# The order of batch 1's transpositions, of the w_out loads and of GpSimd's first sums in a fused attention and MoE kernel

## The chip, the cores and the metric

The kernel runs on one NeuronCore of a Trainium2 chip. The metric is the device time of one execution in microseconds (us); the figure compared is the median of several executions. Engines are named as in the profile: PE (TensorE), PEld (its weight loads), DVE (VectorE), ACT (ScalarE), POOL (GpSimd) and SP (SyncE, which here only issues DMAs).

## The reference

For each of 8 batches and 8 heads, `x` (512 x 64) and `state` (32 x 64) attend to each other. With `scale = 1/sqrt(64)`:

```
a      = softmax(scale * x @ state.T)    # 512 x 32
xread  = a @ state
a2     = softmax(scale * state @ x.T)    # 32 x 512
sread  = a2 @ x
rows   = concat([xread, sread])          # 544 rows a batch, heads side by side: 512 wide
out    = leaky_relu(rows @ w_in, 0.01) @ w_out     # w_in 512 x 2048, w_out 2048 x 512
```

The output has 8 * 544 = 4352 rows of 512 values in fp32.

## The kernel before, in words

**Tiling.** All products run on bf16 operands with fp32 sums. A batch is transposed so that the features lie on the partitions: the tile `xT`. Its scores `sc` (`a_scores`, line 252) are 8 small matmuls on parts of the array. The matrix `M` is `state @ w_in` for one batch, so that the first MoE layer is `M` against the first probabilities `aT`. `M` is made in four column blocks (`a_m`, line 409, and `m_evict`, line 429). The first layer is `ff1` (line 439): two matmuls for each of the 16 row blocks `s`, into a PSUM bank `ph`, and a leaky ReLU on ACT that writes a block of `hT`. The second layer is `piece(b, hT, i, jq, js)` (line 541): for row tile `i`, matmuls over the blocks `4*jq + js` of `hT` and `w_out`, one for each block, into a bank `py` or `pyw`. Line 1005 names `half`, the two halves (0, 1) and (2, 3) of such a quarter.

**Softmax of one batch.** For the first probabilities DVE runs `a_shift` (the maxima `mrow`, line 266; their spread `sh`, line 274; the difference, line 280), ACT runs the exponential (`a_exp`, line 284), DVE runs `a_recip` (lines 289 to 298) and `a_probs` (line 302), which writes `aT`. For the second probabilities DVE runs `a_max2` (line 341), ACT `a_exp2` (line 347, with the row sums) and DVE `a_probs2` (lines 355 to 365), which writes `a2`.

**Order.** There is no scheduler: each engine runs its instructions in the order in which the code issues them, and waits on semaphores. Nothing on an engine passes a waiting instruction, but weight loads may be issued ahead of the matmuls that they belong to.

**Stages around the change.** Batch 0 has its own path (lines 871 to 992). While its `hT` (`h0`) is multiplied by `w_out` in `piece`s, batch 1 (`a1`) is prepared: its `x`, loaded in two halves `x1[0]` and `x1[1]` (line 876), is cast to bf16 on DVE (line 995), transposed on PE by 8 small matmuls for each half into a PSUM tile `pxt2` (line 1015) and copied to `xT` on DVE (line 1018). Then come `a_scores(a1)`, the softmax of batch 1, and from line 1066 on the loop of `ff1(a1, h1, s)`, which needs `aT` of batch 1 and carries the rest of batch 0's `piece`s between its steps.

Batch 2's `x` comes in two halves `xl` and is cast on ACT (line 126, called at line 1041); each half is then transposed by a DMA that SP issues (`a_xt_half`, line 239). The states of batches 2 and 3 are loaded by 8 DMAs of SP (`load_state(0)`, line 199, which follow a memset of two columns, line 999), cast on POOL (`state_cast(0)`, line 208) and transposed by a third DMA of SP (`state_t(0)`, line 213). `a_scores(a2)` at line 1077, step 4 of the loop, needs all three of these.

**Queues.** `w_in`, `w_out` (with a cast from fp32 to bf16), `x1` and `xl` are loaded by DMAs that POOL issues (lines 144 to 156 and 871 to 885), and they land in the order of their issue. Later loads, transposing DMAs and the output are issued by SP. POOL also forms differences of blocks of `w_out` (`tw_sum`, line 577), of which `tw_sum(1, ...)` at line 1029 needs `w_out` tiles 0 to 7.

Of the kernel before, what the change touches and what calls it, by code (L numbers as in the profile page):

```python
# [9 lines left out]
P = 128  # L10
B, H, S, D = 8, 8, 512, 64
# [4 lines left out]
NT = S // P  # L16
NK = H // 2
SCALE = 1.0 / (D ** 0.5)

BF16 = mybir.dt.bfloat16  # L20
# [7 lines left out]
def kernel(  # L28
# [9 lines left out]
    nc = tc.nc  # L38

    consts = ctx.enter_context(tc.tile_pool(name="consts", bufs=1))  # L40
# [6 lines left out]
    psum = ctx.enter_context(tc.tile_pool(name="psum", bufs=2, space=bass.MemoryType.PSUM))  # L47
# [5 lines left out]
    VEC, SCA, POO = nc.vector.tensor_copy, nc.scalar.copy, nc.gpsimd.tensor_copy  # L53
# [18 lines left out]
    ident = consts.tile([P, P], BF16, name="ident")  # L72
# [47 lines left out]
    def pair_of(a, t, k):  # L120
        h = 2 * (k % 2)
        return a.xb[k // 2][:, t, h:h + 2, :].rearrange("p h d -> p (h d)")
# [27 lines left out]
    def load_w_out_rows(j0, j1):  # L150
        nc.gpsimd.dma_start(
            w_out_bf[:, j0:j1, :], moe_w_out[P * j0:P * j1, :].rearrange("(j p) f -> p j f", p=P)
        )

    def load_w_out(c):
        load_w_out_rows(4 * c, 4 * (c + 1))
# [39 lines left out]
    stf = [consts.tile([P, hi - lo, P], FP32, name=f"stf{lo}") for lo, hi in groups]  # L196
    stb = [consts.tile([P, hi - lo, P], BF16, name=f"stb{lo}") for lo, hi in groups]

    def load_state(i):
        lo, hi = groups[i]  # L200
        for k in range(NK):
            for g in range(2):
                nc.sync.dma_start(
                    stf[i][NS * k:NS * (k + 1), :, D * g:D * (g + 1)],
                    state[lo:hi, 2 * k + g].rearrange("b n d -> n b d"),
                )
# [38 lines left out]
    def st_of(a, g, k):  # L245
        rows = slice(D * g, D * (g + 1))
        if a.b == 0:
            return stbd[rows, k, g ^ (k // 2), :]
        t = st1 if a.b == 1 else st_t[0][:, a.b - 2] if a.b < 4 else st_t[1][:, a.b - 4]
        return t[rows, NS * k:NS * (k + 1)]  # L250

    def a_scores(a):
        sc = psum.tile([P, 2, S], FP32, name="sc", tag="sc", bufs=1)
        for k in range(NK):
            for g in range(2):
                nc.tensor.matmul(  # L256
                    sc[NS * k:NS * (k + 1), g, :],
                    lhsT=st_of(a, g, k),
                    rhs=a.xTh[k // 2][D * g:D * (g + 1), :, k % 2, :],
                    start=True, stop=True,  # L260
                )
        a.sc = sc
# [52 lines left out]
    def a_shift(a):  # L315
        a_max(a)
        a_diff(a)
# [36 lines left out]
    def a_probs2(a):  # L354
        nc.vector.tensor_scalar(out=a.r2[:], in0=a.r2[:], scalar1=1e-9, scalar2=None, op0=ALU.add)
        q2 = att.tile([P, 2], FP32, name="qc", tag="qc")
        nc.vector.reciprocal(q2[:], a.r2[:])
        if a.b in (0, 6):
            pairs[a.b] = att.tile([P, 2, 2, S], BF16, name="a2p", tag="a2p", bufs=1)
        if a.b in (0, 1, 6, 7):  # L360
            a.a2 = pairs[a.b - a.b % 2][:, a.b % 2]
        else:
            a.a2 = att.tile([P, 2, S], BF16, name="a2", tag="a2", bufs=1)[:]
        for g in range(2):
            nc.vector.tensor_scalar(
                out=a.a2[:, g, :], in0=a.e2[:, g, :],
                scalar1=q2[:, g:g + 1], scalar2=None, op0=ALU.mult,
            )
# [172 lines left out]
    def piece(b, hT, i, jq, bank=None, copy=SCA, js=range(4)):  # L541
        if jq == 0 and js[0] == 0:
            y = ys[b, i] = Y()
            y.py = psum.tile([P, DM], FP32, name="py", tag="py")[:] if bank is None else bank
        y = ys[b, i]
        for j in [4 * jq + v for v in js]:
            nc.tensor.matmul(  # L547
                y.py, lhsT=hT[:, j, P * i:P * (i + 1)], rhs=w_out_bf[:, j, :],
                start=(j == 0), stop=(j == 15),
            )  # L550
        if jq == 3 and copy is not None:
            y_store(b, i, copy)

    def y_store(b, i, copy):
        tag = ("ysb", "s1", "ysb", "s6")[i]
        ysb = ypool.tile([P, DM], FP32, name="ysb", tag=tag, bufs=3 if tag == "ysb" else 1)
        copy(ysb[:], ys[b, i].py)
        nc.sync.dma_start(rows_of(b)[i], ysb[:])
# [5 lines left out]
    def tw_open():  # L564
        for n in (1, 2):
            t = consts.tile([P, HJ, HN], BF16, name=f"tw{n}", tag=f"x1{n - 1}")
            tw[n] = [t[:, 4 * u:4 * (u + 1)] for u in range(2)]
        for n in (3, 4):
            tw[n] = []
            for u in range(2):  # L570
                t = consts.tile([P, 4, HN], BF16, name=f"tw{n}", tag=f"xf{2 * (n - 3) + u}")
                tw[n].append(t[:])
# [199 lines left out]
    a0, a1, a2 = att_of[:3]  # L772
# [102 lines left out]
    for u in range(2):  # L875
        nc.gpsimd.dma_start(
            x1[u][:], x[1, NK * u:NK * (u + 1)].rearrange("h (p t) d -> p h (t d)", t=NT)
        )
    load_w_out_rows(2, 4)
    load_w_out(1)  # L880
    load_w_out(2)
    load_x_half(2, 0)
    load_w_out_rows(12, 14)
# [52 lines left out]
    h0 = hpool.tile([P, 16, S], BF16, name="hT", tag="hT")  # L936

    def open_ff1_0(tag):
        if tag in ("sc", "big"):
            pr = psum.tile([P, 2, S], FP32, name="php", tag=tag, bufs=1)  # L940
            return pr, [pr[:, 0], pr[:, 1]]
        ph = [psum.tile([P, S], FP32, name="ph", tag=tag) for _ in range(2)]
        return ph, [p[:] for p in ph]
# [39 lines left out]
    for j, tag in ((4, "ph"), (6, "big"), (8, "py"), (10, "big"), (12, "py"), (14, "ph")):  # L983
        t, bk = open_ff1_0(tag)
# [5 lines left out]
        elif j == 8:  # L990
            a_scores(a0)
            m_halves(a0, 3, "ph")
            a_max2(a0)
    for u in range(2):
        VEC(
            a1.xb[u].rearrange("p t h d -> p h t d"),
            x1[u][:].rearrange("p h (t d) -> p h t d", t=NT),
        )
    nc.vector.memset(stf[0][:, 0, D - 1:D + 1], 0.0)
    load_state(0)  # L1000

    for g in range(2):
        a_exp2(a0, g)
    wide = psum.tile([P, 2, DM], FP32, name="pyw", tag="big", bufs=1)
    half = (range(0, 2), range(2, 4))
    for u in range(2):
        piece(0, h0, 2 + u, 0, bank=wide[:, u], js=half[0])
    for i in (0, 1):
        piece(0, h0, i, 0, js=half[0])
    for u in range(2):  # L1010
        ps = psum.tile([P, NT, 2, P], BF16, name="pxt2", tag="ph")
        for t in range(NT):
            for v in range(2):
                h = NK * u + 2 * v
                nc.tensor.transpose(
                    ps[:, t, v, :], pair_of(a1, t, h // 2), ident[:]
                )
        VEC(a1.xT[:, :, 2 * u:2 * u + 2, :], ps[:])
    for i in (2, 3):
        piece(0, h0, i, 0, js=half[1])  # L1020
    a_scores(a1)
    m_evict(a1, 1, a_m(a1, 1, "ph"), SCA)
    for i in (0, 1):
        piece(0, h0, i, 0, js=half[1])
    a_probs2(a0)
    a_shift(a1)
    a_max2(a1)
    tw_open()
    for j in (4, 6, 0, 2):
        tw_sum(1, j, j + 2, nc.gpsimd)  # L1030
    for i in (0, 1):
        piece(0, h0, i, 1)
    pm = a_m(a1, 2, "ph")
    a_exp(a1)
    m_evict(a1, 2, pm, SCA)
# [93 lines left out]
    for b in range(2, B):  # L1129
# [22 lines left out]
        for s in range(16):  # L1152
# [75 lines left out]
            if b == 7 and s in FA_AT:  # L1228
                i = FA_AT.index(s)
# [49 lines left out]
    for n in (1, 2, 6, 5, 7, 3, 4):  # L1279
        two_product(q, n)  # L1280
        if n in (3, 4):
            u = n - 3
# [43 lines left out]
```

## Time and profile before

| what | us |
|---|---|
| median of 3 executions | 202.36 (202.03 to 202.39) |
| the profiled execution | 202.76 |
| its span, from the first to the last instruction | 201.0 |
| PE busy in the span | 195.4 (97%) |
| DVE busy | 158.7 (79%) |
| ACT busy | 141.9 (71%) |
| POOL busy | 72.6 (36%) |

All times in traces count from the first instruction of the program. In the timeline, a row is a run of like instructions on one engine: start, length from the first start to the last end, engine, line, operation, output and input, number, and in brackets the idle time before it with what ended it. The length that a matmul shows includes its way through the array, so that neighbouring matmuls overlap in the rows; their distance is that of their starts. The chain of waits leads from the last instruction back through whatever released each step; there each row holds the time that counts towards the end. The DMA view gives for each issue the size and the time from issue to landing.

### The profile page before, as it was taken

What the parts mean: (1) busy time and instruction counts of PE and PEld (TensorE: products, weight loads), DVE (VectorE), ACT (ScalarE), POOL (GpSimd) and SP (SyncE); (2) the same over time, 40 slices, a digit from 0 to 9 for tenths busy, and PEclk for the clock granted to TensorE, in tenths of its full rate; (3) what the DMA queues carried; (4) which work ended last, traced back from release to release, by engine and by line L of the source; (5) the groups of instructions that cost most, each with busy time, mean ns of one, the idle gap of its engine ahead of it and who ended that gap; (6) DMA issues with size and microseconds to landing.
All of it is one profiled execution on the core that took longest, in us unless ns stands there. A gap on an engine that the chain in (4) does not pass through costs nothing.

```text
span 201.0 us, 4628 instructions
## 1 busy us (share of the span) xinstructions
PE 195.4 (97%) x1880; PEld 130.1 (65%) x1880; DVE 158.7 (79%) x241; ACT 141.9 (71%) x274; POOL 72.6 (36%) x76
## 2 busy tenths in 40 slices
PE   7998999999999999999999999999999999999993
PEld 3643534443476767776776677676767777799982
DVE  3665799399999989985999889898999945984712
ACT  3678738899889868766887779777868555757420
POOL 8823272992091373037300760054004600540000
PEclk9999999999999999999999999999999999999999
DMA  6999998697999944852473404220025302210115
GB/s 198 207 207 297 212 290 147 119 346 170 196 219 228 308 49 72 237 216 55 88 225 139 128 16 92 104 109 0 0 104 157 58 0 104 108 49 8 52 38 170
DMA packets 38773, 27.75 MB, mean 138 GB/s; under 512 B 24416, under 2 KB 35808, under 8 KB 38752
## 3 DMA queue, kind: packets, MB, share of 16 engines
q1 hardware_dynamic: 33584, 20.78, 39.3%
q0 software_dynamic: 4832, 6.29, 15.4%
q10 hardware_dynamic: 336, 0.39, 0.8%
q8 instruction: 14, 0.23, 0.5%
q14 instruction: 7, 0.06, 0.1%
HBM read 17.30 MB, written 8.91 MB: 130 GB/s over the span
## 4 chain that ended last, share of the span: by engine, by line
PE 91%; DMA 3%; DVE 2%; ACT 1%; ACTq 1%; SPq 0%; issue 0%
PE ph L442 24%; PE ppx L642 18%; PE ppb L642 15%; PE py L547 7%; PE ppr L699 6%; PE pm L421 4%; PE pyw L547 3%; PE pf L520 3%; PE ppw L642 3%; DMA xf<-in_x_dram 2%; PE psr L394 2%; PE php L947 1%; PE ph L947 1%; PE sc L256 1%; DMA out_dram<-ysb 1%; DVE m L830 1%
## 5 line engine op out<-in xcount | busy, mean ns | idle before, releaser
L447 ACT ACTIVATE hT<-ph 128x512 bf16<-128x512 f32 x112 | 66.7, 605 | 25.2 <-PE ph L442 24.5
L442 PE MATMUL ph<-aT,M 128*128 128x512 bf16 x224 | 65.5, 380 | 0.0
L607 POOL TENSOR_TENSOR S<-hT,S 128x512 bf16<-128x512 bf16 x24 | 32.1, 1357 | 82.2 <-DVE S L607 55.5
L642 PEld LDWEIGHTS <-S 128*128 128x128 bf16 x384 | 37.0, 98 | 12.7 <-issue 0.9
L642 PEld LDWEIGHTS <-hT 128*128 128x128 bf16 x288 | 28.0, 98 | 11.1
L607 DVE TENSOR_TENSOR S<-hT 128x1024 bf16<-128x1024 bf16 x24 | 25.0, 1069 | 3.3 <-ACT hT L447 3.3
L442 PEld LDWEIGHTS <-M 128*128 128x128 bf16 x224 | 20.9, 98 | 8.8 <-issue 2.9
L642 PE MATMUL ppx<-tw,S 128*128 128x256 bf16 x160 | 20.8, 273 | 0.0
L547 PEld LDWEIGHTS <-hT 128*128 128x128 bf16 x96 | 9.1, 98 | 11.4 <-issue 1.0
L547 PE MATMUL py<-w_out_bf,hT 128*128 128x512 bf16 x64 | 16.0, 380 | 0.0
L739 DVE TENSOR_TENSOR ysb<-ppb,s 128x512 f32<-128x512 f32 x12 | 8.3, 692 | 6.2 <-PE ppb L642 6.1
L642 PE MATMUL ppb<-tw,S 128*128 128x256 bf16 x96 | 12.4, 273 | 0.0
L642 PE MATMUL ppb<-w_out_bf,hT 128*128 128x256 bf16 x96 | 12.4, 273 | 0.0
L642 PE MATMUL ppb<-w_out_bf,S 128*128 128x256 bf16 x96 | 12.3, 273 | 0.0
L435 ACT CAST M<-pm 128x1024 bf16<-128x1024 f32 x11 | 11.2, 1018 | 0.3 <-PE pm L421 0.3
L642 PE MATMUL ppx<-w_out_bf,hT 128*128 128x256 bf16 x80 | 11.2, 273 | 0.0
L347 ACT ACTIVATE e<-sc,mcol 128x512 bf16<-128x512 f32 x16 | 11.1, 700 | 0.0
L586 POOL TENSOR_TENSOR tw<-w_out_bf 128x512 bf16<-128x512 bf16 x8 | 9.0, 1153 | 4.2 <-DMA w_out_bf<-in_moe_w_out_dram 4.2
L642 PE MATMUL ppx<-tw,hT 128*128 128x256 bf16 x80 | 10.4, 273 | 0.0
L341 DVE TENSOR_REDUCE mcol<-sc 128x2 f32<-128x1024 f32 x8 | 9.7, 1214 | 0.0
L266 DVE TRANSPOSE_TENSOR_REDUCE mrow<-sc 128x32 f32<-128x1024 f32 x7 | 8.7, 1242 | 1.2 <-PE sc L256 1.2
L132 POOL CAST xb<-xl 128x2048 bf16<-128x2048 f32 x5 | 9.5, 1892 | 0.0
(148 smaller groups left out, 322.5 us busy)
## 6 DMA issues: line engine op xcount, KB each, us to landing
out_dram<-ysb SPq DMA_DIRECT2D x11, 512.0 KB, 2.6
xl<-in_x_dram SPq DMA_DIRECT2D x5, 1024.0 KB, 6.4
out_dram<-ysb SPq DMA_DIRECT2D x9, 256.0 KB, 4.7
w_in_bf<-in_moe_w_in_dram POOLq DMA_DIRECT2D x4, 512.0 KB, 9.8
xf<-in_x_dram SPq DMA_DIRECT2D x4, 256.0 KB, 3.7
w_out_bf<-in_moe_w_out_dram POOLq DMA_DIRECT2D x4, 256.0 KB, 13.6
x<-in_x_dram POOLq DMA_DIRECT2D x2, 512.0 KB, 14.6
w_out_bf<-in_moe_w_out_dram POOLq DMA_DIRECT2D x2, 512.0 KB, 16.5
```

Source lines behind the costliest of these rows:

```text
L132: nc.gpsimd.tensor_copy(xt[b][:].rearrange("p t h d -> p h t d"), xl[b][:].rearrange("p h (t d) -> p h t d", t=NT),)
L266: nc.vector.tensor_reduce(out=m1[:], in_=flat.rearrange("p (c j) -> p c j", j=NS), axis=AX.X, op=ALU.max, apply_transpose=True,)
L341: nc.vector.tensor_reduce(out=a.m2[:], in_=a.sc[:], axis=AX.X, op=ALU.max, negate=True)
L347: nc.scalar.activation(out=a.e2[:, g], in_=a.sc[:, g, :], func=AF.Exp, bias=a.m2[:, g:g + 1], accum_out=a.r2[:, g:g + 1],)
L435: copy(a.M[:, :, cols], pm[:])
L442: nc.tensor.matmul(ph[:], lhsT=a.M[:, g, P * j:P * (j + 1)], rhs=a.aT[:, g, :], start=(g == 0), stop=(g == 1),)
L447: nc.scalar.activation(out=hT[:, j, :], in_=ph[:], func=AF.Prelu, scale=1 / SCALE, alpha=0.01)
L547: nc.tensor.matmul(y.py, lhsT=hT[:, j, P * i:P * (i + 1)], rhs=w_out_bf[:, j, :], start=(j == 0), stop=(j == 15),)
L586: eng.tensor_tensor(out=tw[n][u][:, at], in0=in0, in1=in1, op=ALU.subtract)
L607: eng.tensor_tensor(out=part(n), in0=in0, in1=in1, op=op)
L642: nc.tensor.matmul(q[bank][v], lhsT=lhsT, rhs=w_of(n, j), start=q["open", bank] and j == 0, stop=j == 7, skip_group_check=True,)
L699: nc.tensor.matmul(q.bank[w], lhsT=lhsT, rhs=w_of(n, j), start=n in (1, 2, 5) and j == 0, stop=j == HJ - 1, skip_group_check=True,)
```

## The change

Four things move; no arithmetic changes.

1. The loads of `w_out` on POOL's queue. Before, tiles 2 and 3 followed both halves of batch 1's `x`, and tiles 4 to 7 came as one DMA. Now tiles 2 and 3 lie between the two halves of `x`, tiles 4 and 5 follow the second half, and tiles 6 and 7 are a DMA of their own.
2. The cast, the 8 transposing matmuls and the copy of each half of batch 1's `x` are three functions, and the two halves are no longer issued together: the first half's transpositions follow the first eight `piece` matmuls; then come all eight of `half[1]` of the first quarter, the second half's transpositions, four matmuls of the second quarter, and only then `a_scores(a1)`.
3. On DVE, the memset of `stf[0]` (which SP's eight loads of `load_state(0)` wait for) follows the first copy, the second half's cast follows that, and `a_probs2(a0)` lies between the second half's cast and its copy.
4. POOL copies one element of batch 0's second probabilities into a new tile `behind` before its first `tw_sum`, so that these sums wait until `a_probs2(a0)` is done.

The counts of matmuls, of DVE and of ACT instructions stay the same. POOL has one DMA issue and one copy more.

```diff
@@ -876,8 +876,8 @@
             x1[u][:], x[1, NK * u:NK * (u + 1)].rearrange("h (p t) d -> p h (t d)", t=NT)
         )
-    load_w_out_rows(2, 4)
-    load_w_out(1)
+        load_w_out_rows(2 + 2 * u, 4 + 2 * u)
+    load_w_out_rows(6, 8)
     load_w_out(2)
@@ -991,14 +991,26 @@
-    for u in range(2):
+    def x1_cast(u):
         VEC(
             a1.xb[u].rearrange("p t h d -> p h t d"),
             x1[u][:].rearrange("p h (t d) -> p h t d", t=NT),
         )
-    nc.vector.memset(stf[0][:, 0, D - 1:D + 1], 0.0)
-    load_state(0)
-
+
+    def x1_t(u):
+        ps = psum.tile([P, NT, 2, P], BF16, name="pxt2", tag="ph")
+        for t in range(NT):
+            for v in range(2):
+                h = NK * u + 2 * v
+                nc.tensor.transpose(
+                    ps[:, t, v, :], pair_of(a1, t, h // 2), ident[:]
+                )
+        return ps
+
+    def x1_copy(u, ps):
+        VEC(a1.xT[:, :, 2 * u:2 * u + 2, :], ps[:])
+
+    x1_cast(0)
     for g in range(2):
         a_exp2(a0, g)
@@ -1007,29 +1019,27 @@
     for i in (0, 1):
         piece(0, h0, i, 0, js=half[0])
-    for u in range(2):
-        ps = psum.tile([P, NT, 2, P], BF16, name="pxt2", tag="ph")
-        for t in range(NT):
-            for v in range(2):
-                h = NK * u + 2 * v
-                nc.tensor.transpose(
-                    ps[:, t, v, :], pair_of(a1, t, h // 2), ident[:]
-                )
-        VEC(a1.xT[:, :, 2 * u:2 * u + 2, :], ps[:])
-    for i in (2, 3):
+    x1_copy(0, x1_t(0))
+    nc.vector.memset(stf[0][:, 0, D - 1:D + 1], 0.0)
+    load_state(0)
+    x1_cast(1)
+    a_probs2(a0)
+    for i in (2, 3, 0, 1):
         piece(0, h0, i, 0, js=half[1])
+    x1_copy(1, x1_t(1))
+    for i in (0, 1):
+        piece(0, h0, i, 1, js=half[0])
     a_scores(a1)
     m_evict(a1, 1, a_m(a1, 1, "ph"), SCA)
-    for i in (0, 1):
-        piece(0, h0, i, 0, js=half[1])
-    a_probs2(a0)
     a_shift(a1)
     a_max2(a1)
     tw_open()
+    behind = consts.tile([1, 1], BF16, name="behind")
+    nc.gpsimd.tensor_copy(behind[:], a0.a2[:1, 1, S - 1:])
     for j in (4, 6, 0, 2):
         tw_sum(1, j, j + 2, nc.gpsimd)
     for i in (0, 1):
-        piece(0, h0, i, 1)
+        piece(0, h0, i, 1, js=half[1])
     pm = a_m(a1, 2, "ph")
     a_exp(a1)
```

## The prediction

> **What bounds the kernel now.** I read the page first: PE is the engine that carries the span.
>
> ```profile
> PE 195.4 (97%) x1880; PEld 130.1 (65%) x1880; DVE 158.7 (79%) x241; ACT 141.9 (71%) x274; POOL 72.6 (36%) x76
> ```
>
> So the change can gain only where PE waits, and it loses wherever it makes PE wait. Next the chain of waits around the changed lines (start, us that count towards the end):
>
> ```profile
> 21.47 0.86 PE pyw L547 x4
> 22.33 0.86 PE py L547 x4
> 23.19 0.89 PE pxt L1015 x16
> 24.09 0.86 PE pyw L547 x4
> 24.95 0.47 PE sc L256 x8
> 25.41 0.22 PE pm L421 x8
> 25.63 2.69 PE py L547 x12
> ...
> 35.68 0.86 PE ph L442 x4
> ```
>
> From 21.47 to 35.68 it never leaves PE. A `piece` matmul counts 0.86/4 = 0.216 us, a transposition 0.89/16 = 0.056. So I look for steps that are longer than their like. The timeline of PE (starts) has one, batch 1's scores against batch 2's:
>
> ```profile
> 23.92 1.03 PE L547 MATMUL pyw<-w_out_bf,hT 128*128 128x512 bf16 x4
> 24.88 0.54 PE L256 MATMUL sc<-xT,st 64*32 64x512 bf16 x8
> 25.56 0.39 PE L547 MATMUL py<-w_out_bf,hT 128*128 128x512 bf16 x1
> ```
> ```profile
> 39.50 0.41 PE L256 MATMUL sc<-xT,st_t 64*32 64x512 bf16 x8
> 40.05 0.39 PE L442 MATMUL ph<-aT,M 128*128 128x512 bf16 x1
> ```
> ```profile
> 35.52 0.38 PE L442 MATMUL ph<-aT,M 128*128 128x512 bf16 x1
> ```
>
> Scores and the block of M behind them take 25.56 - 24.88 = 0.68 for batch 1 and 40.05 - 39.50 = 0.55 for batch 2: 0.13 is lost. DVE tells why:
>
> ```profile
> 22.52 0.69 DVE L995 CAST xb<-x 128x1024 bf16<-128x1024 f32 x1 [0.56 <-DMA x<-in_x_dram]
> 23.68 1.29 DVE L1018 COPY xT<-pxt 128x1024 bf16<-128x1024 bf16 x2 [0.45 <-PE pxt L1015]
> 24.88 0.16 DVE L355 TENSOR_SCALAR r<-r 128x2 f32<-128x2 f32 x1
> 25.81 1.24 DVE L266 TRANSPOSE_TENSOR_REDUCE mrow<-sc 128x32 f32<-128x1024 f32 x1
> 33.87 0.69 DVE L302 TENSOR_TENSOR aT<-e,qb 128x1024 bf16<-128x1024 bf16 x1
> ```
>
> The second copy to `xT` ends at 23.68 + 1.29 = 24.97, just behind the scores' start at 24.88. **That 0.13 is all there is to gain here.** The reader should also note the last two rows: batch 1's softmax starts on DVE at 25.81 and `aT` is there at 33.87 + 0.69 = 34.56, while `ff1(a1)` starts on PE at 35.52. Less a semaphore of some 0.05 (the copy's end at 24.97 to the scores' second half), the slack is 0.91.
>
> **Part 1, the loads.** Issues on POOL's queue and their times to landing (rows in pairs):
>
> ```profile
> 7.56 0.79 POOL L876 DMA_DIRECT2D x<-in_x_dram  x1
> x<-in_x_dram POOLq DMA_DIRECT2D x1, 512.0 KB, 14.9
> 8.31 0.75 POOL L151 DMA_DIRECT2D w_out_bf<-in_moe_w_out_dram  x1
> w_out_bf<-in_moe_w_out_dram POOLq DMA_DIRECT2D x1, 256.0 KB, 15.3
> 9.85 0.78 POOL L151 DMA_DIRECT2D w_out_bf<-in_moe_w_out_dram  x1 [0.79 <-DMA w_in_bf<-in_moe_w_in_dram]
> w_out_bf<-in_moe_w_out_dram POOLq DMA_DIRECT2D x1, 512.0 KB, 16.3
> ```
>
> The second half of x lands at 22.5, tiles 2-3 at 23.6, tiles 4-7 at 26.15: 1.1 to 1.25 us for two tiles. With the same bytes in another order, tiles 2-3 land near 22.2, the second half of x at 23.6, tiles 4-5 at 24.85, tiles 6-7 at 26.15. POOL's extra issue costs it 0.75 at a time when it waits for older transfers anyway (idle 0.79 in the row above).
>
> [...]
>
> **Part 2, PE's order.** I lay the instructions out anew with the starts of before. The eight first `piece` matmuls end their slots at 23.03 as before (the 16 transpositions, 0.89, follow them and end where `pyw` starts, at 23.92). Then: 8 transpositions to 23.48, 8 matmuls (1.73) to 25.21, 8 transpositions to 25.65, 4 matmuls (0.86) to 26.52, the change to small tiles (24.88 less 23.92 + 4 x 0.216 = 0.09), **scores at 26.61**, 1.73 later than now. What each step needs is there: tiles 2-3 (22.2 against 23.48), tiles 4-5 (24.85 against 25.65), tiles 6-7 (26.15 against about 27.6).
>
> **Part 3, DVE's order.** The first copy starts at 23.68 as now and a copy holds DVE for about 0.61 (the two 1.29, less an overlap of 0.08); memset; the second cast at 24.34, with x since 23.6; it ends at 25.03, 0.15 ahead of its transpositions. `a_probs2(a0)` then holds DVE from 24.95 for 25.81 - 24.88 = 0.93, to 25.88. The second group of transpositions ends at about 25.85, so the copy runs from 25.88 to 26.57. The scores at 26.61 need not wait: the 0.13 goes. But the maxima follow the scores: batch 2 has its maxima here:
>
> ```profile
> 39.98 1.25 DVE L266 TRANSPOSE_TENSOR_REDUCE mrow<-sc 128x32 f32<-128x1024 f32 x1 [1.22 <-PE sc L256]
> ```
>
> That is 39.98 - 39.50 = 0.48 behind the scores' start, so for batch 1 they come at 26.61 + 0.48 = 27.09, **1.28 later than 25.81**: before, DVE was behind on the probabilities and hid part of PE's order; now PE is late. From there the chain is serial (maxima, spread, difference, exponential, sums, reciprocal, spread, product) and nothing in it was waiting for anything else, so `aT` moves from 34.56 to 35.84. PE, 0.13 early, would want `ff1(a1)` at 35.39 and gets it at 35.84 + 0.05 = 35.89 to 35.91: a wait of 0.52, and **+0.39 against before**. This wait holds the loop's first matmul, and on PE's in-order queue all of `ff1`, batch 0's last pieces and batch 2's scores behind it.
>
> **Behind it: ACT and SP.** ACT runs the exponential, then M, then the casts of batch 2's x:
>
> ```profile
> 29.62 1.06 ACT L284 ACTIVATE e<-sh 128x1024 bf16<-128x1024 f32 x1 [2.88 <-DVE sh L280]
> 31.52 1.06 ACT L126 CAST xb<-xl 128x1024 bf16<-128x1024 f32 x1
> 33.41 1.04 ACT L126 CAST xb<-xl 128x1024 bf16<-128x1024 f32 x1 [0.83 <-DMA xl<-in_x_dram]
> 36.15 1.09 ACT L447 ACTIVATE hT<-ph 128x512 bf16<-128x512 f32 x2 [0.34 <-PE ph L442]
> ```
>
> The exponential moves by 1.28 and the first cast with it, to end at 33.86; the second only to 33.77-34.81, since it used to wait 0.83 for its transfer. Before, ACT was done with what lies between that cast and the first ReLU at 36.15 - 0.34 = 35.81; now, 0.36 later, at 36.17, and the ReLU comes at 36.15 + 0.39 = 36.54: hidden. SP's three transposing DMAs follow:
>
> ```profile
> 32.60 2.05 SPq L240 DMA_TRANSPOSE xT<-xb  x1
> 34.76 1.24 SPq L240 DMA_TRANSPOSE xT<-xb  x1
> 36.10 1.19 SPq L214 DMA_TRANSPOSE st_t<-stb  x1
> st_t<-stb SPq DMA_TRANSPOSE x1, 2.9
> q0 software_dynamic: 30, 0.03, 10.2%
> 89.45 1.23 SPq L372 DMA_TRANSPOSE a2T<-a  x1
> 39.49 0.11 PEld L256 LDWEIGHTS <-st_t 64*32 64x32 bf16 x8 [0.42 <-DMA st_t<-stb]
> ```
>
> The states land at 36.10 + 2.9 = 39.0, and PE wants them at 39.49 (its 0.42 idle is the usual change of tiles, not a wait): slack 0.49. In the changed kernel PE wants them at 39.88. Their issue stands third in SP's queue: 33.88, plus the first issue, plus 1.24, plus 0.21 of semaphores (34.76 - 34.65 and 36.10 - 36.00). The first took 2.05 where an equal one with a quiet queue took 1.23 (row of 89.45): two ends for a cost that I cannot settle. With 1.23 the states land at 33.88 + 1.23 + 1.24 + 0.21 + 2.9 = 39.46, in time; with 2.05 at 40.28, and PE waits 40.33 - 39.88 = 0.45 more. From 33.0 to 34.7 the DMA view still shows the last 30 packets of POOL's queue (q0) beside it; 1.28 later they are gone, so I take 1.23.
>
> **Part 4, POOL.** `behind` waits for the probabilities, done near 25.96, when tiles 4-5 are there and 6-7 about to be: the sums start near where tiles 4-7 let them start before, and their reader on DVE stands behind the product for `aT`: nothing. The memset comes 1.2 later (24.3 for 23.2), and SP's state loads with it; POOL casts what they bring:
>
> ```profile
> 32.85 0.86 POOL L209 TENSOR_SCALAR stb<-stf 128x256 bf16<-128x256 f32 x1 [2.06 <-DVE qh L296]
> ```
>
> It ended at 33.71, ends at 34.9 if all of the 1.2 comes through, and is wanted by the third issue at 33.88 + 1.23 + 1.24 + 0.21 = 36.56: hidden.
>
> **Sum.** -0.13 (scores) + 0.52 (`aT`) = +0.39 on PE from 35.5 on. After that PE is dense and the order is unchanged, so the shift reaches the end. The profiled execution would go from 202.76 to 203.15. The median of the runs is 0.40 lower than that execution: 202.36 + 0.39 = **202.75**.
>
> **Rivals.**
>
> *The states are late too.* The first transposing issue keeps its 2.05. Total +0.39 + 0.45 = +0.84: 203.2. For: the row does not say what held that issue, and 30 packets are few. Against: the quiet 1.23.
>
> *Faster.* If `w_out` comes more slowly in ordinary executions than in the profiled one, the kernel before waits for tiles 4-7, which PE wants at about 26.44 and which land at 26.15, while the changed one wants tiles 4-5 only (0.8 of slack) and 6-7 at 27.6. With these 1.2 later, before loses 0.9 and the changed kernel still 0.39: 202.36 - 0.5 = 201.9 in relative terms. It decides from a landing later than 26.15 + 0.29 + 0.39 = 26.8. Against: no PE wait for `w_out` in the trace, and three runs within 0.36.
>
> *The change does not do what it says.* `aT` is later by less, or the slack of 0.91 is larger by jitter of either, and PE only sheds its 0.13: 202.2 to 202.5.
>
> *The split costs a landing.* If the extra DMA delayed all behind it by a step of its own, 1.1 to 2.5 us as between the landings above, batch 2's second half would land at 34.5 to 35.9 and its cast end 1.05 later, at 35.55 to 36.95, where the second transposing issue would go at 35.22. The states then land 0.33 to 1.73 later, at 39.8 to 41.2, and PE waits up to 1.35 for them: 202.75 to 204.1. The landings speak against it. [...]
>
> **Chances.** Forecast 0.53 (own range 202.55 to 203.0); states late 0.24; faster 0.08; no effect 0.13; the split's landing 0.02. A measurement can tell about 0.2%, 0.4 us, from no change. The forecast lies at that edge: half of it counts as slower, half as within. Slower: 0.27 + 0.24 + 0.02 = 0.53; within: 0.26 + 0.13 = 0.39; faster 0.08. The range takes in the forecast, the states' delay and most of "no effect": 202.3 to 203.4.
>
> **What would show it.** Right: scores of batch 1 at about 26.6 and the first block of M right behind (0.55); maxima at 27.1; `aT` done at 35.8, with PE's weight loads for `ff1` idle some 0.5 until then; the first transposing issue about 1.2 long, batch 2's scores at 39.9. Wrong: a PE wait for x or `w_out` between 23 and 28; an idle PE ahead of batch 2's scores; `ff1(a1)` at 35.5 or earlier.

## The result, and the profile after

The changed kernel takes 202.65 us (median of 22 executions, 202.45 to 204.28) and the kernel before 202.16 (22 executions, 201.99 to 202.89). The ratio is 1.0024, with a 95% interval of 1.0013 to 1.0035: the change costs about half a microsecond.

The two profiled executions seem to deny that. That of the changed kernel took 202.73, with this span and PE on its page:

```profile
span 200.9 us, 4604 instructions
PE 194.4 (97%) x1853; PEld 130.4 (65%) x1880; DVE 159.5 (79%) x241; ACT 142.0 (71%) x274; POOL 73.2 (36%) x78
```

That is 0.1 less than the span of before. (PE's 1853 for 1880 are missing records, not missing work.) The reason stands ahead of all that was changed. PE's timeline of the kernel before has its first `pyw` matmul here:

```profile
21.30 1.03 PE L547 MATMUL pyw<-w_out_bf,hT 128*128 128x512 bf16 x4
```

and PE's timeline of the changed kernel goes (left out: matmuls in between that keep their places):

```profile
20.75 1.03 PE L547 MATMUL pyw<-w_out_bf,hT 128*128 128x512 bf16 x4
...
22.47 0.61 PE L1005 MATMUL pxt<-ident,xb 128*128 128x128 bf16 x8
...
24.65 0.61 PE L1005 MATMUL pxt<-ident,xb 128*128 128x128 bf16 x8
25.09 1.03 PE L547 MATMUL py<-w_out_bf,hT 128*128 128x512 bf16 x4
26.05 0.41 PE L256 MATMUL sc<-xT,st 64*32 64x512 bf16 x8
...
26.61 1.04 PE L547 MATMUL py<-w_out_bf,hT 128*128 128x512 bf16 x3
27.57 0.69 PE L421 MATMUL pm<-w_in_bf,st 64*32 64x512 bf16 x8
28.20 1.90 PE L547 MATMUL pyw<-w_out_bf,hT 128*128 128x512 bf16 x8
...
34.26 1.03 PE L547 MATMUL py<-w_out_bf,hT 128*128 128x512 bf16 x4
35.35 1.04 PE L442 MATMUL ph<-aT,M 128*128 128x512 bf16 x4
```

The changed one starts its `piece`s 0.55 earlier. Of PE's waits up to there, the one that differs most is that of its weight loads for blocks of `w_in` (line 421), which both kernels load alike: 1.3 in the kernel before, 0.4 in the changed one. It is not always this transfer: the kernel before, unchanged and profiled again, waited 0.4 for `w_in`, but 1.4 for the cast of batch 0's x (line 784), and started at 21.02. The kernels below started between 20.45 and 21.80 (one at 24.43). So the comparison of two traces has to be made from an anchor behind those first transfers. I take the start of that first `pyw` matmul and call it T0. From T0, the end of the span lies at 179.68 in the kernel before (200.98 - 21.30), at 179.69 in its second profile, and at **180.20** in the changed kernel (200.95 - 20.75): +0.52, against +0.49 between the medians. `ff1(a1)` starts at T0 + 14.22 before and T0 + 14.60 after: +0.38 of the +0.52 is there at the point that the prediction looked at.

DVE's timeline of the changed kernel, from the second probabilities of batch 0 to `aT`:

```profile
24.74 0.62 DVE L365 TENSOR_SCALAR a2p<-e,qc 128x512 bf16<-128x512 bf16 x2
25.29 0.69 DVE L1011 COPY xT<-pxt 128x1024 bf16<-128x1024 bf16 x1
26.53 1.25 DVE L266 TRANSPOSE_TENSOR_REDUCE mrow<-sc 128x32 f32<-128x1024 f32 x1 [0.55 <-PE sc L256]
...
34.60 0.69 DVE L302 TENSOR_TENSOR aT<-e,qb 128x1024 bf16<-128x1024 bf16 x1
```

The second copy ends at 25.98 and the scores start at 26.05: no loss there any more. But DVE now stands idle 0.55 until the scores come, and `aT` is there at 35.29, 0.06 ahead of `ff1(a1)`. The waits of PE's weight loads name it (total, times, longest):

```profile
PEld L442 <- DVE aT L302: 0.6, 1, 0.6
```

And the chain of waits, which before did not leave PE between 21.47 and 35.68, leaves it now exactly for batch 1's softmax:

```profile
26.12 0.39 PE sc L256 x8
...
26.53 1.26 DVE mrow L266
...
34.60 0.70 DVE aT L302
...
35.35 0.62 PE ph L442 x2
```

### The profile page after: what moved, and what is told of

It reads as the page before. It is cut to its first block, busy times and chain, and to the rows that moved or that the text cites. A ratio compares the mean times of both kernels' runs of the same rounds, so it can differ in the third digit from the quotient of the medians.

```text
span 200.9 us, 4604 instructions
## 1 busy us (share of the span) xinstructions
PE 194.4 (97%) x1853; PEld 130.4 (65%) x1880; DVE 159.5 (79%) x241; ACT 142.0 (71%) x274; POOL 73.2 (36%) x78
## 4 chain that ended last, share of the span: by engine, by line
PE 77%; DVE 13%; ACT 3%; DMA 3%; issue 2%; ACTq 1%
PE ph L442 18%; PE ppx L642 18%; PE ppb L642 15%; PE ppr L699 5%; PE pf L520 3%; PE pm L421 3%; PE ppw L642 3%; PE ph L947 2%; DVE sh L274 2%; PE psr L394 2%; DVE mrow L266 2%; DMA xf<-in_x_dram 2%; PE py L547 2%; DVE qb L298 1%; DVE r L289 1%
## 5 line engine op out<-in xcount | busy, mean ns | idle before, releaser
L442 PE MATMUL ph<-aT,M 128*128 128x512 bf16 x202 | 60.9, 379 | 0.2
L289 DVE TRANSPOSE_TENSOR_REDUCE r<-e 128x32 f32<-128x1024 bf16 x7 | 8.7, 1244 | 0.7 <-ACT e L330 0.5
```

The costliest lines, as they stand in the source:

```text
L289: nc.vector.tensor_reduce(out=r1[:], in_=e1[:].rearrange("p (c j) -> p c j", j=NS), axis=AX.X, op=ALU.add, apply_transpose=True,)
L442: nc.tensor.matmul(ph[:], lhsT=a.M[:, g, P * j:P * (j + 1)], rhs=a.aT[:, g, :], start=(g == 0), stop=(g == 1),)
```

## The experiments

The theory under test is the prediction's: the later scores delay `aT` one for one, PE waits for it, and the rest of the change is hidden. Its rivals: it is the loads, or GpSimd's part, or the profile's equal spans tell the truth and nothing changed. All profiles against the kernel before, by time and from T0. Each ratio is taken against executions of the kernel before from the same session, whose medians were 202.16 to 202.39, so that the times of two rows need not compare as their ratios do:

| kernel | T0 | T0 to `ff1(a1)` | T0 to end, less 179.68 | us | ratio to before, 95% |
|---|---|---|---|---|---|
| after | 20.75 | 14.60 | +0.52 | 202.65 | 1.0024 (1.0013 to 1.0035) |
| before_again | 21.02 | 14.21 | +0.01 | 202.6, one execution | |
| e1_fill2 | 21.23 | 14.80 | +0.52 | 202.98 | 1.0036 (1.0018 to 1.0054) |
| e2_later | 20.79 | 15.47 | +1.37 | 203.83 | 1.0073 (1.0052 to 1.0093) |
| e3_loads | 20.65 | 15.80 | +1.73 | 204.04 | 1.0084 (1.0063 to 1.0105) |
| e4_order | 21.22 | 14.61 | +0.52 | 203.52 | 1.0062 (1.0039 to 1.0085) |
| e4_again | 20.69 | 15.47 | +1.41 | 203.6 | 1.0056 (1.0040 to 1.0073) |
| e5_half | 20.49 | 14.09 | -0.15 | 202.35 | 1.0001 (0.9985 to 1.0016) |
| e6_free | 20.54 | 18.21 | +3.98 | 205.28 | 1.0144 (1.0108 to 1.0180) |
| e8_swap | 20.45 | 15.00 | +0.78 | 202.90 | 1.0033 (1.0020 to 1.0045) |
| e9_loads_behind | 24.43 | 14.22 | +0.01 | 203.21 | 1.0050 (1.0030 to 1.0070) |
| e9_again | 21.80 | 14.52 | +0.29 | 203.13 | 1.0032 (1.0017 to 1.0047) |
| e10_early | 20.70 | 14.93 | +0.70 | 202.98 | 1.0038 (1.0019 to 1.0057) |

One us is 0.5% here. Where a profile's T0 is an ordinary one, most ratios follow the column before them; the exceptions are told below.

### e1_fill2: work moved into the wait

The changed kernel, with two matmuls of the loop brought ahead of it:

```diff
+    piece(0, h0, 2, 3, copy=None, js=half[1])
     for s in range(16):
         ff1(a1, h1, s)
...
-                piece(0, h0, i, 3, copy=None, js=half[1])
+                if i != 2:
+                    piece(0, h0, i, 3, copy=None, js=half[1])
```

> The changed kernel, with the two matmuls of batch 0's piece 2 that stood behind step 1 of ff1(a1) moved ahead of step 0. If PE loses its time waiting for aT at step 0 (0.52 us), these 0.43 us of work fit into the wait: 0.43 us faster than the changed kernel, within 0.1 us of the kernel before (ratio 1.000). If the loss lies elsewhere (an extra DMA, the order of the loads, POOL), nothing is gained: ratio 1.002 as for the changed kernel.

Measured: no gain; the end lies at T0 + 180.20 as in the changed kernel, and the interval of its ratio contains the change's 1.0024. The two matmuls take 0.43, and `ff1(a1)` starts 0.20 later than in the changed kernel (T0 + 14.80 against 14.60). So PE had only 0.23 of wait left there, not the 0.52 of the prediction; what became of the rest shows in e2_later. Even the 0.23 does not reach the end. PE's timeline has batch 2's scores and the first `ppr` behind batch 3's scores here:

```profile
39.62 0.41 PE L256 MATMUL sc<-xT,st_t 64*32 64x512 bf16 x8
...
55.17 1.03 PE L699 MATMUL ppr<-w_out_bf,hT 128*128 128x256 bf16 x8
```

The scores are at T0 + 18.39, 0.20 earlier than in the changed kernel (39.34, T0 + 18.59), but the `ppr` is at T0 + 33.94 as there (54.69). Something between them holds PE at the same time in both; it is followed up in e8_swap.

### e2_later: the scores later still

The changed kernel with the whole second quarter ahead of the scores, four matmuls (0.86) more:

```diff
     for i in (0, 1):
-        piece(0, h0, i, 1, js=half[0])
+        piece(0, h0, i, 1)
     a_scores(a1)
...
-    for i in (0, 1):
-        piece(0, h0, i, 1, js=half[1])
```

> The changed kernel, with four more piece matmuls (0.86 us) put ahead of batch 1's scores. If each step later of the scores is passed on through batch 1's softmax to step 0 of ff1(a1), the wait there grows by 0.86: 1.25 us slower than the kernel before (ratio 1.006), and PE waits 1.4 us for aT. If the scores' place does not matter, the work of PE is only put in another order: ratio 1.002 as for the changed kernel.

Measured: scores at T0 + 6.17 (0.87 later than in the changed kernel), `ff1(a1)` 0.87 later, the end 0.85 later. The delay goes through one for one, as it must if `aT` sets `ff1(a1)`. But this run alone does not separate `aT` from a second path that moves with the scores, since PE's timeline of this kernel also has a wait that the prediction had not (e3_loads and e8_swap below separate the two):

```profile
27.18 0.40 PE L421 MATMUL pm<-w_in_bf,st 64*32 64x512 bf16 x8
28.28 0.90 PE L421 MATMUL pm<-w_in_bf,st 64*32 64x512 bf16 x8 [0.70 <-ACT M L433]
```

`a_m(a1, 2)` (second row) uses the `ph` banks of `a_m(a1, 1)` (first row) and must wait until ACT has copied them out. Before, twelve matmuls lay between the two and covered that; in the changed kernel it is four (26.61 to 27.57 above, where the row shows three of them), so `a_m(a1, 2)` runs from 27.57 to 28.20, 0.63 where it took 0.34 in the kernel before (28.26 to 28.60). ACT's timeline of the changed kernel shows until when it is held:

```profile
26.74 1.07 ACT L433 CAST M<-pm 128x512 bf16<-128x512 f32 x2 [3.21 <-PE pm L421]
```

0.29 of PE's wait is thus taken here, ahead of the softmax's end, and 0.23 at `ff1(a1)`: 0.52 together, in two places.

### e3_loads: the loads alone

The kernel before with part 1 only:

```diff
-    load_w_out_rows(2, 4)
-    load_w_out(1)
+        load_w_out_rows(2 + 2 * u, 4 + 2 * u)
+    load_w_out_rows(6, 8)
```

> The kernel before with the new order of the w_out and x1 loads alone. If landings go by bytes, the second half of x lands about 0.9 us later than in the kernel before, its cast holds back both copies on DVE and PE waits for the second group of transpositions by about 0.6: 0.45 to 0.6 us slower than before (ratio 1.002 to 1.003). If the order of the loads does not matter here: ratio 1.000.

Measured: +1.73 from T0, far more than the later second half of x explains. POOL's and DVE's timelines of this kernel:

```profile
24.02 4.71 POOL L586 TENSOR_TENSOR tw<-w_out_bf 128x512 bf16<-128x512 bf16 x4 [1.54 <-DMA w_out_bf<-in_moe_w_out_dram]
```
```profile
24.85 0.35 DVE L355 TENSOR_SCALAR r<-r 128x2 f32<-128x2 f32 x1
...
25.44 2.29 DVE L365 TENSOR_SCALAR a2p<-e,qc 128x512 bf16<-128x512 bf16 x2
27.64 1.24 DVE L266 TRANSPOSE_TENSOR_REDUCE mrow<-sc 128x32 f32<-128x1024 f32 x1
```

With tiles 4 and 5 there at 24.0 instead of after 26, POOL's first sums start ahead of `a_probs2(a0)`, and DVE's two products for `a2p` take 2.29 beside them instead of 0.62. The maxima, behind them in DVE's queue, come at T0 + 6.99 (before: T0 + 4.51), 2.48 later. PE's timeline shows what that does:

```profile
36.45 1.04 PE L442 MATMUL ph<-aT,M 128*128 128x512 bf16 x4 [0.79 <-DVE aT L302]
```

`ff1(a1)` is 1.58 later than before, that is 2.48 less a slack of 0.90, almost the 0.91 of the prediction. Here the maxima do not wait for the scores, which start at 24.99, and `a_m(a1, 2)` does not wait for its banks (28.24 to 28.59, 0.35). So **that `aT` sets `ff1(a1)` is shown without the second path**. The earlier loads do not stand alone: this is what `behind` is for.

### e6_free: the changed kernel without `behind`

```diff
-    behind = consts.tile([1, 1], BF16, name="behind")
-    nc.gpsimd.tensor_copy(behind[:], a0.a2[:1, 1, S - 1:])
```

> The changed kernel without the one-element copy that holds GpSimd's sums behind the second probabilities. If GpSimd and VectorE lock each other out while a sum runs, the sums that start with tiles 4-5 stretch the second probabilities on DVE from 0.62 to about 2.3 us as in the run with the loads alone, the second copy and the scores come 1.5 to 2 us later: 1.9 to 2.5 us slower than before (ratio 1.010 to 1.012). If the engines do not disturb each other: ratio 1.002 as for the changed kernel.

Measured: dearer than expected, +3.98 from T0 (3.46 more than the change), for two reasons. The first is that the products also stand ahead of the second copy to `xT`. DVE's timeline:

```profile
24.13 1.12 DVE L355 TENSOR_SCALAR r<-r 128x2 f32<-128x2 f32 x1
...
25.49 2.25 DVE L365 TENSOR_SCALAR a2p<-e,qc 128x512 bf16<-128x512 bf16 x2
27.66 0.68 DVE L1011 COPY xT<-pxt 128x1024 bf16<-128x1024 bf16 x1
```

The second half of the scores waits until 28.39, T0 + 7.85, 2.55 later than the scores of the changed kernel. The second reason is PE's granted clock in this profile, which was lower for a time behind that wait. PE's timeline, and from the page the granted clock in tenths, in slices of 5.1 us:

```profile
28.39 0.40 PE L256 MATMUL sc<-xT,st 64*32 64x512 bf16 x4 [2.15 <-DVE xT L1011]
...
28.94 1.60 PE L547 MATMUL py<-w_out_bf,hT 128*128 128x512 bf16 x4
...
31.03 2.70 PE L547 MATMUL pyw<-w_out_bf,hT 128*128 128x512 bf16 x8
```
```profile
PEclk9999987999999999999999999999999999999999
```

By single microseconds the granted clock was 0.63, 0.50, 0.50 and 0.66 from 29 to 33, and 1.00 ahead of that and behind it (0.990 over the whole execution). From the start of these two rows to the next row PE needs 1.53 and 2.54 us, in the changed kernel 0.96 and 1.74: 1.37 lost. `aT` is there at 37.60, but `ff1(a1)` starts only at 38.75, so that in this profile `aT` no longer sets it. An estimate from these rows: at full clock `ff1(a1)` would follow `aT` by 0.06, at 37.66, and the loss against the kernel before would be 1.09 smaller, 2.9. The timing is wide (203.97 to 206.39) and its median gives less, 1.44% or 2.99, than the profiled execution, which took 206.01.

Not every DVE instruction was stretched beside POOL's sums, which run here from 24.06 to 28.75. The small one (128 x 2) takes 1.12 against 0.16 undisturbed, about the length of one of the sums (4.69 for four), and ends at 25.25, about when the first of them ends (24.06 + 4.69/4 = 25.23); the two products take 2.25 against 0.62. But the second copy to `xT` keeps its length beside the sums: 0.68 here, and 0.69 in the changed kernel, where they start at 25.57. What makes the difference no run shows.

### e9_loads_behind and e9_again: loads and `behind`, without the new order

e3_loads with the two lines of `behind` put back; the same kernel twice.

> The kernel before with the new order of the loads and the one-element copy ahead of GpSimd's sums. If the loads cost by themselves through the later second half of x, PE waits 0.5 to 0.7 for the second transpositions: 0.45 to 0.65 us slower than before (ratio 1.002 to 1.003), and the second probabilities take 0.62 again. If the 1.8 us of the run with the loads alone lay in the transfers, it stays at ratio 1.008.

Measured: in the first profile PE came to its `piece`s 3 us late (T0 at 24.43), x had long been there, and nothing was lost: 14.22, as before. This execution took 205.89, the longest of its seven. Its PE waited 2.09 for `w_in` up to 14.40, and from 15 to 18 the granted clock was 0.50 (0.992 over the whole execution). Therefore the second:

> The kernel before with the new order of the loads and the one-element copy, once more, since PE's start was late by 3 us in the profile of the first run. From the first piece matmul to the first matmul of ff1(a1): 14.7 to 14.9 us if the later second half of x holds the second transpositions (14.22 in the kernel before), 14.2 if the loads cost nothing by themselves.

Measured: T0 is 21.80, late too, but part of the loss shows. PE's timeline:

```profile
24.39 0.62 PE L1015 MATMUL pxt<-ident,xb 128*128 128x128 bf16 x8 [0.25 <-DVE stf L999]
```

The second eight transpositions wait 0.25 for the second cast (the row names the memset right behind it), because the second half of x lands behind `w_out` tiles 2 and 3; in e3_loads, with T0 at 20.65, this wait was 0.60. The end is +0.29; the timing, whose executions are not tied to that late start, gives 1.0032 and 1.0050. So `behind` takes most of the +1.73 of e3_loads away, and what the trace still shows is the later x. Whether the whole 0.7 to 1.0 us of the timings is this wait, no profile with an early start shows. Taken alone, the loads are a loss even with `behind`.

### e4_order and e4_again: the new order with the old loads

The changed kernel with part 1 undone, twice:

```diff
-        load_w_out_rows(2 + 2 * u, 4 + 2 * u)
-    load_w_out_rows(6, 8)
+    load_w_out_rows(2, 4)
+    load_w_out(1)
```

> The changed kernel with the old order of the loads (tiles 4 to 7 in one DMA behind both halves of x). If tiles 4 to 7 land about 4.8 us behind the first piece matmul as in the kernel before, the four matmuls of the second quarter wait 0.5 us, the scores behind them come 0.5 later and aT with them: 0.85 us slower than before (ratio 1.004). If the loads do not matter: ratio 1.002 as for the changed kernel.

Measured: from T0 the trace is that of the change (14.61, +0.52), but the timing is 1.0062, well above the change's 1.0024. T0 was late, 21.22. The same again:

> The changed kernel with the old order of the loads, once more: the timed runs were 0.8 us slower than the changed kernel while the profile showed the same 14.6 us from the first piece matmul to ff1(a1). If that loss is a wait for tiles 4 to 7, a profile in which PE starts early shows more than 14.6 there; if it lies ahead of the first piece matmul, that matmul starts at 21.2 again, against 20.5 to 20.8 in other kernels.

Measured, with T0 at 20.69, on PE's timeline:

```profile
23.36 1.02 PE L547 MATMUL pyw<-w_out_bf,hT 128*128 128x512 bf16 x4 [0.34 <-DMA w_out_bf<-in_moe_w_out_dram]
...
25.90 1.02 PE L547 MATMUL py<-w_out_bf,hT 128*128 128x512 bf16 x4 [0.21 <-DMA w_out_bf<-in_moe_w_out_dram]
```

Two waits for `w_out`, first tiles 2 and 3, then tiles 4 to 7: from T0 the first row starts 0.50 later than in the changed kernel, the second 0.87. Scores come at T0 + 6.16, `ff1(a1)` at 15.47, the end at +1.41, and the timing says the same as the first time (1.0056). With an early start the new order needs the new loads, and it is the timing, with many starts, that had shown it first.

### e10_early: is it the four matmuls ahead of the scores?

The changed kernel without the four matmuls of the second quarter ahead of the scores:

```diff
-    for i in (0, 1):
-        piece(0, h0, i, 1, js=half[0])
     a_scores(a1)
...
     for i in (0, 1):
-        piece(0, h0, i, 1, js=half[1])
+        piece(0, h0, i, 1)
```

> The changed kernel without the four matmuls of the second quarter ahead of batch 1's scores (they follow, as in the kernel before). If those four matmuls are what makes the scores late, the scores come 0.86 earlier and the wait for aT goes: within 0.1 of the kernel before (ratio 1.000). If the second copy of xT, behind the later second cast and the second probabilities on DVE, sets the scores, they stay 5.3 us behind the first piece matmul, PE waits there and has the four matmuls still to do ahead of ff1(a1): 0.3 to 0.65 slower than the changed kernel (ratio 1.004 to 1.006).

Measured, on PE's timeline:

```profile
25.14 0.40 PE L256 MATMUL sc<-xT,st 64*32 64x512 bf16 x4
26.00 0.40 PE L256 MATMUL sc<-xT,st 64*32 64x512 bf16 x4 [0.46 <-DVE xT L1011]
```

The first half of the scores comes 0.86 earlier (T0 + 4.44), but the second half stands at T0 + 5.30 as in the changed kernel, held by the second copy to `xT`. `ff1(a1)` is 0.33 later than in the changed kernel, the end 0.18 later. So the four matmuls do not delay the scores: they fill a gap that **DVE's order** (second cast, `a_probs2`, second copy) leaves.

### e5_half: only the 0.13

The kernel before, with one thing moved: four matmuls of the first quarter from behind the scores to ahead of them, to cover the second copy.

```diff
-    for i in (2, 3):
+    for i in (2, 3, 0, 1):
         piece(0, h0, i, 0, js=half[1])
     a_scores(a1)
     m_evict(a1, 1, a_m(a1, 1, "ph"), SCA)
-    for i in (0, 1):
-        piece(0, h0, i, 0, js=half[1])
```

> The kernel before, with all eight matmuls of half[1] of the first quarter ahead of batch 1's scores (four more than before, 0.86 us), loads and DVE order as before. If only the 0.9 us between aT and step 0 of ff1(a1) counts, 0.86 us of later scores minus the 0.4 that DVE spends on the second probabilities anyway fits in, and the 0.13 us that PE waited for the second copy of xT goes: 0.1 us faster than the kernel before (ratio 0.9995), which the trace can show from the first piece matmul to the end and the timing cannot tell from no change. If every step later of the scores costs its own length, 0.4 to 0.9 us slower (ratio 1.002 to 1.004).

Measured: `ff1(a1)` 0.13 earlier, the end 0.15 earlier. The 0.13 of the prediction was there to be had, with the loads, the casts and the transpositions left as they were. DVE waits a little for the scores, and `aT` still comes before PE wants it:

```profile
25.41 1.25 DVE L266 TRANSPOSE_TENSOR_REDUCE mrow<-sc 128x32 f32<-128x1024 f32 x1 [0.33 <-PE sc L256]
```

In the trace this version beats both; the timing cannot tell it from the kernel before (1.0001, 0.9985 to 1.0016).

### e8_swap: the other 0.14

Behind `ff1(a1)` the changed kernel loses 0.14 more (+0.38 there, +0.52 at the end). POOL and DVE, batch 2, first before, then after, from their timelines:

```profile
44.65 1.89 POOL L132 CAST xb<-xl 128x2048 bf16<-128x2048 f32 x1
```
```profile
46.76 0.18 DVE L293 TENSOR_SCALAR r<-r 128x32 f32<-128x32 f32 x1
```
```profile
35.98 4.87 POOL L586 TENSOR_TENSOR tw<-w_out_bf,tw 128x512 bf16<-128x512 bf16 x4 [2.06 <-DVE tw L586]
...
45.25 1.90 POOL L132 CAST xb<-xl 128x2048 bf16<-128x2048 f32 x1
```
```profile
46.61 0.58 DVE L293 TENSOR_SCALAR r<-r 128x32 f32<-128x32 f32 x1
```

In POOL's order the second group of sums (35.98) waits for a sum that DVE makes behind `aT`, so with `aT` later by 1.28 it runs later, and the cast of batch 3's x at its end with it. Before, that cast ended at 46.54, ahead of DVE's 46.76; now it ends at 47.15, and DVE's small instruction, started at 46.61, lasts until 47.19. From T0, it ends at 25.64 before and at 26.44 after: half of the 0.80 is PE's shift, half the collision. In e1_fill2 DVE comes to it earlier, and it lasts the longer, to T0 + 26.44 again (46.89 + 0.78 - 21.23):

```profile
46.89 0.78 DVE L293 TENSOR_SCALAR r<-r 128x32 f32<-128x32 f32 x1
```

How that reaches PE shows 7 us later, at a cast of M on DVE and the first `ppr` on PE, again first before, then after:

```profile
53.70 0.68 DVE L1127 CAST M<-pm 128x512 bf16<-128x512 f32 x1
54.72 1.04 PE L699 MATMUL ppr<-w_out_bf,hT 128*128 128x256 bf16 x8
```
```profile
53.95 0.68 DVE L1137 CAST M<-pm 128x512 bf16<-128x512 f32 x1
54.69 1.03 PE L699 MATMUL ppr<-w_out_bf,hT 128*128 128x256 bf16 x8
```

From T0 the cast ends 0.80 later, as the small instruction did. Before, the `ppr` started 0.34 behind that end; now it starts 0.06 behind it. PE's shift of 0.38 and the 0.28 of slack cover 0.66 of the 0.80, and 0.14 is left. The theory: the collision holds both kernels at the same time and takes the 0.20 that e1_fill2 had gained; without it the 0.14 is won back. The edit swaps the two groups of POOL's sums, so that the one without DVE's sum goes first:

```diff
-    for n in (4, 3):
+    for n in (3, 4):
```

> The changed kernel with GpSimd's third sums ahead of the fourth, so that it does not wait for DVE's second sums and its cast of batch 3's x ends some 1 us earlier. If the small DVE instruction at line 293 of batch 2 (0.58 us against 0.18 before) was held by that cast, it is 0.18 again, batch 2's aT comes 0.4 earlier and PE's second wait near 53 us (0.12) goes: ratio 1.002 or a little less. If that row was slow for another reason, it stays at 0.58.

Measured, on POOL's and DVE's timelines:

```profile
33.69 5.83 POOL L586 TENSOR_TENSOR tw<-w_out_bf 128x512 bf16<-128x512 bf16 x4
```
```profile
34.30 1.07 DVE L302 TENSOR_TENSOR aT<-e,qb 128x1024 bf16<-128x1024 bf16 x1
...
46.69 0.18 DVE L293 TENSOR_SCALAR r<-r 128x32 f32<-128x32 f32 x1
```

The cause of the 0.58 is confirmed (0.18 again), but POOL's sums now meet batch 1's `aT`: 1.07 instead of 0.69. `ff1(a1)` is 0.40 later than in the changed kernel and the end 0.26: the collision was moved to a dearer place. That hides what was won: `ff1(a1)` is 0.78 later than in the kernel before, and the end is 0.78 later too, so that behind `ff1(a1)` nothing is lost any more. The cast of M ends at 54.32 and the `ppr` starts at 54.66, 0.34 apart as before. **So the removal does show that the 0.14 was this collision.** The other kernels agree (by the table, the end's delay less that of `ff1(a1)`): where the small instruction takes 0.56 to 0.58 (after, e2_later, e3_loads, e4_order, e4_again) 0.12 to 0.16 is lost behind `ff1(a1)`; where it takes 0.18 to 0.22 (e5_half, e6_free, both e9, e10_early) it is within 0.02 of nothing.

The run also says once more what sets `ff1(a1)`: up to `ff1(a1)` PE's rows are those of the changed kernel, `aT` is there 0.38 later than in it, and `ff1(a1)` comes 0.40 later.

### before_again: the anchor

> The kernel before, for a second profile. If the 0.55 us by which its first piece matmul started later than that of the changed kernel is the spread of the first transfers and not an effect of the change, it may start anywhere from 20.5 to 21.3, and from there to the end it is again 179.7 us.

Measured: T0 at 21.02 against 21.30, and from there 14.21 and 179.69 against 14.22 and 179.68. The spread lies ahead of T0; behind it the same code repeats to 0.01.

## Why the prediction was right, and where its steps were off

**The sum held, and by its own mechanism.** +0.39 was forecast at `ff1(a1)`, +0.38 came, and `aT` set it. That 202.65 also came close to the forecast 202.75 is partly luck: the median of the kernel before came out 0.20 below the 202.36 that the sum started from, while the change cost 0.49 and not 0.39. By its steps:

| step | forecast | measured from the rows above |
|---|---|---|
| part 2: scores behind the first `pyw` matmul | 5.31 | 26.05 - 20.75 = 5.30 |
| scores to maxima | 0.48 | 26.53 - 26.05 = 0.48 |
| part 3: `aT` against before | +1.28 | (34.60 - 20.75) - (33.87 - 21.30) = +1.28 |
| scores wait for the second copy | none | none |
| wait of PE | 0.52, at `ff1(a1)` | 0.29 at `a_m(a1, 2)`, 0.23 at `ff1(a1)` |
| behind `ff1(a1)` | 0 | +0.14 |

**Part 1, the loads, held.** No PE wait for x or `w_out` came between 23 and 28. By POOL's issues and their times to landing in the changed kernel, tiles 2-3 were there at 21.40, the second half of x at 22.79, tiles 4-5 at 23.88 and tiles 6-7 at 25.17: in the forecast order, and from T0 0.25 to 0.43 earlier than forecast. The split delayed nothing behind it either: the second half of batch 2's x landed at 32.18, T0 + 11.43, against 33.40, T0 + 12.10, before. The rival of a lost landing falls. The prediction's text costed the loads as neutral, though; e3_loads and e4_again show that they are not neutral alone, only together with the other parts.

**Part 2 named one of two causes.** The prediction put the later scores down to PE's order, with the second copy 0.04 ahead of them. e10_early shows that there was no room at all: with four matmuls fewer ahead of the scores their second half still starts at T0 + 5.30, since DVE's order (second cast, `a_probs2`, second copy) sets the same time. One order alone would not bring `aT` forward. (In part 3, 25.21 - 25.03 is 0.18, not 0.15; nothing hangs on it.)

**The wait was put in one place.** The step "PE, 0.13 early, would want `ff1(a1)` at 35.39" laid PE's matmuls out without the PSUM banks: `a_m(a1, 2)` waits for ACT once only four matmuls cover the eviction. The net is the same, because PE waits for `aT` in the end, but 0.52 of work would not have fitted into that wait: e1_fill2's 0.43 already made `ff1(a1)` later by 0.20.

**"After that PE is dense and the order is unchanged, so the shift reaches the end"** failed by 0.14, the collision of POOL's cast with DVE's reciprocal steps for batch 2 (e8_swap). Part 4 looked at POOL's sums for DVE's readers, not for where POOL's later work would fall on DVE's.

**Part 4's "nothing" held for the change**, but its reason was thin: it did not see that without `behind` the sums would start 1.3 us earlier from T0 (24.06 - 20.54 against 25.57 - 20.75) and stop DVE (e6_free).

**SP's issues.** The choice of 1.23 over 2.05 for the first transposing DMA was right. SP's issues in the changed kernel:

```profile
33.34 2.71 SPq L240 DMA_TRANSPOSE xT<-xb  x2
36.15 1.20 SPq L214 DMA_TRANSPOSE st_t<-stb  x1
```

The first issue took 1.33 of the 2.71, where before the two went from 32.60 to 36.00. With 2.8 from the third issue's start to its landing the states are there at 38.95, ahead of the scores of batch 2 at 39.34. The rival of late states falls.

**The other rivals.** "Faster" falls: no profile of the old loads in the old order shows a wait for `w_out`. e4_again does show such waits, but they come from the new order. "No effect" falls with the interval, which starts at 1.0013. The forecast had said that half of it would be within 0.2%; the ratio of 1.0024 lies just outside, and its interval reaches to both sides.

**Open.** Each kernel has one profile, or two, while the medians are over many starts, so a ratio and its trace can differ by what T0 brings (e4_order, e9_loads_behind). What makes the first transfers (`w_in`, batch 0's x) land earlier or later was not tried, nor what made the granted clock fall in e6_free and e9_loads_behind. Nor was a version with `aT` taken off PE's path altogether.

## What to carry to other kernels

Where an engine is dense, look for who has slack against it: a chain that runs one for one on a second engine (here 0.91 of slack, and 1.28 of delay spent on it) turns a better order on the first engine into a wait. Lay PE's instructions out with their PSUM banks too, since matmuls moved away from between two uses of a bank uncovered its eviction here (0.29 of wait at `a_m(a1, 2)`). Look where work of a third engine falls when a wait moves it: here a cast on POOL, some 11 us behind the start of `ff1(a1)`, cost a quarter of the loss. Compare traces from an instruction behind the first transfers, read the granted clock of a stretch before its loss is put down to an order (in e6_free it was at 0.50 for two us), and trust timings over many executions for what depends on the start.

## What the runs showed of the hardware that was not expected

- Some DVE instructions took longer beside GpSimd's work: 0.16 became 1.12 (128 x 2, e6_free) and a pair of products 0.62 became 2.29 (e3_loads) beside a row of GpSimd sums of 1.2 each, and 0.18 became 0.58 (128 x 32, changed kernel) beside a cast of 1.9.
- The start of the `piece`s moved between 20.45 and 21.80, and once to 24.43, over kernels that hardly differ up to there, and by 0.28 between two profiles of the same code. The range of 1.35 is more than the effect measured here.
- In two profiles PE's granted clock was lower for some microseconds behind a wait: in e6_free 0.63, 0.50, 0.50 and 0.66 from 29 to 33, behind a wait of 2.15 that ended at 28.39, and in e9_loads_behind 0.50 from 15 to 18, behind one of 2.09 that ended at 14.40. In e3_loads, with a wait of 0.79, it was 1.00 over the whole execution. Whether the wait causes it no run shows.
